# Block-sparse attention with a gated MoE on one core: weight pieces, key copies and x copies in other places of the order, and 64-column value products

## The chip, the core and the metric

The kernel runs on one core of a Trainium2 chip. The metric is device microseconds of one execution, the median of three runs. The engines are named as in the profile: PE (TensorE matmul), PEld (its weight load), DVE (VectorE), ACT (ScalarE), POOL (GpSimd) and SP (SyncE, which here only issues DMAs).

## What is computed

```python
# B, H, S, D = 4, 8, 768, 64; blocks of 32 rows, 24 of them; w_val, w_out 512x512, conv_w 5x512
scores = q @ k.T / 8                    # kept where the mask holds
mask = |blk_i - blk_j| <= 1, or i or j is the first or the last block, or blk_j is one of 3 sampled for blk_i
x = softmax(scores) @ v                 # all heads side by side: x is 4 x 768 x 512
gate = sigmoid(causal 5-tap convolution of x with conv_w, column by column)
out = (gate * (x @ w_val)) @ w_out
```

## The kernel before

**Units.** Batches 0 and 1 are the first group, 2 and 3 the second. A *place* is a pair of query blocks in both batches of a group; places -1 and -2 are the first and last block of one batch each, which see all keys (the global places). `ORDER` lists 13 places for each group, each place has two units, so there are 52 units; unit n of the text is step n of the main loop (line 887). Units 0 to 25 are the first group, with the global ones at 18 to 21 and places 9 and 10 at 22 to 25.

**A step of the loop.** In step n PE computes the scores of unit n (`scores`, tile `sc`), DVE their row maxima (`mx`), ACT the exponentials (`pe`, four instructions). For unit n-1 PE transposes the exponentials (`pt`, two tiles) and ACT copies each to SBUF (`ptr`); for unit n-2 PE multiplies by the values (`values`, tile `av`, from the own keys' values `va` and the gathered ones `vb`), DVE divides (`rs`, `x`), PE transposes x (`turn`, `xp`) and ACT copies it to `xT` (`finish`). One call of `values` for a place makes 32 matmuls of 32 columns. Every engine works strictly in the order in which the code is written (class `InOrder`), so an instruction that waits holds back all behind it on its engine.

**Queries.** `qc` tiles, 3 of them, come by DMA from SP; ACT scales each (group 0) `SCALE_AHEAD` = 2 units ahead of its first use.

**Weights.** w_val and w_out come as 8 pieces of 512 KB in 64-bit words, each issued by SP in a step set by `WEIGHTS_AT`, into four staging tiles (`wst`) that are later the buffers of xh, xl, yh and yl. `decode` turns one into a high part and a rest: four DVE instructions (`words<-wst`, two on `wst`, `words<-words,wst`), an ACT cast (`wv` or `wo`, high part) and a POOL subtraction (rest). `prepare` advances this in every step of the loop, once behind each of the two `pt` tiles: one DVE instruction in the first half, two in the second, so three a unit; so a piece's cast can come to stand between the two `ptr` copies. Only when all pieces are decoded do the gates of the MoE begin (`gates`, 16 instructions `th` on DVE for a tile of rows, ACT ahead of and behind them).

**The MoE.** When all x of a row tile are in `xT`, it is queued for gates, for its split into xh (ACT) and xl (POOL), and for `project`: products `vp` with w_val, gating on DVE, yh (ACT), yl (POOL), products `op` with w_out. `fill` puts these PE pieces between the attention's from unit 16 on, at the pace of `PACE`.

**Keys.** A place's 12 key blocks stand in `kg` (2 tiles). The group's keys are in SBUF (`keys`); POOL copies from there, except that for places 9 and 10 of the first group and for the first place of the second (`FROM_HBM`) SP fetches the sampled blocks (6 DMAs a place, and 2 more for the second group's first place) from memory. The keys of the second group are loaded in units 22 and 23 (`KEYS_AT`).

Of the kernel before, what the change touches and what calls it, by code (L numbers as in the profile page):

```python
# [22 lines left out]
DV = D + 1  # L23
# [12 lines left out]
ORDER = (1, 2, 0, 3, 4, 5, 6, 7, 8, -1, -2, 9, 10)  # L36
KEYS_AT = (22, 22, 23, 23, 23, 23)
QRING = 3
# [32 lines left out]
def steps(n, half):  # L71
    return 2 if half or n >= 14 else 1

# [5 lines left out]
def attention_moe(ctx, tc, qb, kb, v, vp, sampled, w_val, conv_w, w_out, ident_in, slot_in, out):  # L79
# [140 lines left out]
    decoded = set()  # L220

    def decode_weights():

        yield from decode(cwp[:, 0, :], cwp[:, 1, :], cst, CH * KW)
        dve.tensor_tensor(
            out=cw.rearrange("p c k -> p (c k)"), in0=cwp[:, 0, :].bitcast(F32), in1=cwp[:, 1, :].bitcast(F32),
            op=ALU.add,
        )
        for n in range(2 * CH):
            dst = wv if n < CH else wo  # L230
            while len(staged) <= n or step[0] < staged[n][0] + (DECODE_LAG if n else FIRST_LAG):
                yield False
            yield from decode(dst[0][:, n % CH, :], dst[1][:, n % CH, :], staged[n][1], DM)
            decoded.add(n)
        decoded.add("all")

# [263 lines left out]
    def values(un):  # L500
# [14 lines left out]
        else:  # L515
            slots = [(a, h, b, (4 * a + 2 * b + h) * DV) for a in range(2) for h in range(2) for b in range(2)]
            own = pr.pl.va[:, pr.i]
            rest = pr.pl.vb.rearrange("p j (e d) -> p j e d", e=EACH)[:, :, pr.i]
            for a, h, b, hd in slots:
                for c in range(2):  # L520
                    for j in range(2):
                        rows = slice(64 * b + BLK * j, 64 * b + BLK * j + BLK)
                        vt = rest[:, j, :] if c else own
                        matmul(
                            pr.av[rows, a, h, :], un.PT[4 * h + 2 * a + c][:, rows], vt[:, hd : hd + DV],
                            start=c == 0, stop=c == 1, tile_position=(0, rows.start),
                        )
# [204 lines left out]
    def queue_rows(bt, t):  # L732
        m = Rows()
        m.bt, m.tile, m.w, m.begun, m.pending, m.gated, m.need = bt, t, WIDTHS[t], False, False, 0, 0
        to_gate.append((m, gates(m)))
        to_split.append((m, split(m)))

    def prepared(m):
# [22 lines left out]
    def prepare(steps):  # L761
        for _ in range(steps):
            if next(decoding, None):
                continue

            if to_gate and (to_gate[0][0].begun or len(gating) < 2):
                m = to_gate[0][0]
                if not m.begun:
                    m.begun = True
                    gating.add(id(m))  # L770
                advance(to_gate)

# [114 lines left out]
    for n in range(N + LAG_V):  # L887
        step[0] = n
        if n == 0:
            begin()  # L890
        else:
            while more_queries(n):
                pass
            while more_own(n):
# [12 lines left out]
        if n:  # L907
            until("scaled", n + SCALE_AHEAD, scale, "queries")
        store()
# [5 lines left out]
        if n == 0:  # L915
# [5 lines left out]
            begin_second()  # L921
        until("early", n + COPY_AHEAD, copy_early, "keys")
        if n < AT_ONCE:
# [7 lines left out]
        mine = units[n - LAG_V].pr if 0 <= n - LAG_V < N and units[n - LAG_V].last else None  # L931
        if mine is not None and not any(k >= N or units[k].pl.glob for k in (n + 1, n + 2)) and not completes(mine):
# [18 lines left out]
        if 0 <= n - LAG_T < N:  # L951
            for half, _ in enumerate(transposes(units[n - LAG_T]) if n > LAG_T else range(2)):
                if half == 1:
                    ends_of_pairs()
                for _ in range(2):
# [3 lines left out]
                crowded = half and n > LAG_T and units[n - LAG_T].pl.glob and units[min(n + 1, N - 1)].pl.glob  # L959
                prepare(1 if crowded else steps(n, min(half, 1)))  # L960
                settle()
        else:
            fill()
            ends_of_pairs()
            prepare(steps(n, 0))
# [56 lines left out]
```

## Time and profile before

| | |
|---|---|
| median of 3 runs (369.94, 368.28, 369.55) | 369.55 us |
| the profiled execution | 366.96 us |
| its span | 365.2 us |
| PE busy | 343.1 us, 94% |
| DVE, ACT, POOL busy | 254.0, 241.9, 158.0 us |
| granted TensorE clock, mean | 0.998 |

All durations below are of the profiled execution, which was 2.6 us faster than the median of the runs. PE is the busiest engine by far. In the page's timeline of 40 slices PE's digits are 8 or below only in the first slices, up to about 90 us, and at the end.

### The profile page before, as it was taken

To read this page: it belongs to the slowest core of one execution; us is meant where nothing else is said; L and a number is where in the kernel's file an instruction comes from. 1 tells how busy PE (TensorE), PEld (TensorE's weight loads), DVE (VectorE), ACT (ScalarE), POOL (GpSimd) and SP (SyncE) were. 2 spreads that over 40 slices of the span, in tenths; PEclk is the share of its full clock that TensorE was granted. 3 is DMA by queue.
4 is the path that set the end of the run, shared out by engine and by line. 5 is a ranking of instruction groups with operands and counts; after the bars stand their busy time and mean duration, and the time that the engine had idled before them with its cause. 6 is when DMAs were issued, how large, how long until landed. Compare 5 with 4: busy or idle time off the path is not lost.

```text
span 365.2 us, 15814 instructions
## 1 busy us (share of the span) xinstructions
PE 343.1 (94%) x6628; PEld 270.7 (74%) x6628; DVE 254.0 (70%) x543; ACT 241.9 (66%) x564; POOL 158.0 (43%) x232
## 2 busy tenths in 40 slices
PE   8899888778999999999999999998999999998995
PEld 7576565457877888777787778876779778987883
DVE  4666797968976964399599845698569542989720
ACT  2769696697877875686868766686667855635321
POOL 0373494943235012677248831455004810645540
PEclk9999999999999999999999999999999999999999
DMA  7987888874981798776624666345515001020202
GB/s 271 370 265 270 277 272 274 292 220 113 334 305 44 243 384 242 256 211 196 202 79 145 180 206 208 87 154 203 175 65 177 4 31 61 0 83 4 88 0 87
DMA packets 32122, 64.60 MB, mean 177 GB/s; under 512 B 4659, under 2 KB 16052, under 8 KB 31924
## 3 DMA queue, kind: packets, MB, share of 16 engines
q1 hardware_dynamic: 31762, 63.51, 52.9%
q8 instruction: 52, 0.85, 0.9%
q14 instruction: 18, 0.15, 0.1%
q10 hardware_dynamic: 290, 0.09, 0.1%
HBM read 57.29 MB, written 6.29 MB: 174 GB/s over the span
## 4 chain that ended last, share of the span: by engine, by line
PE 62%; DVE 17%; DMA 7%; ACT 6%; SPq 3%; issue 3%; POOL 1%; ACTq 0%; DVEq 0%; POOLq 0%
PE op L97 15%; PE vp L97 12%; PE av L97 12%; PE pt L97 10%; DVE th L97 10%; PE sc L97 8%; DVE mx L97 4%; DMA qc<-in_q 4%; PE xp L97 3%; DMA wst<-in_w_out 3%; SPq L97 2%; PE s L97 2%; ACT pe L97 2%; ACT ptr L97 2%; DMA wst<-in_w_val 1%
## 5 line engine op out<-in xcount | busy, mean ns | idle before, releaser
L97 DVE SCALAR_TENSOR_TENSOR th<-xT,cw,th 128x388 f32<-128x388 f32 (+1 forms) x128 | 98.2, 782 | 20.6 <-ACT th L97 18.4
L97 POOL COPY kg<-keys 128x256 f32 (+2 forms) x155 | 77.1, 542 | 42.6 <-PE sc L97 15.8
L97 ACT ACTIVATE pe<-sc,mx 128x256 f32<-128x256 f32 x176 | 68.9, 475 | 39.2 <-DVE mx L97 39.0
L97 POOL TENSOR_TENSOR yl<-th,yh 128x384 fp32r<-128x384 f32 x32 | 36.2, 1132 | 116.1 <-ACT yh L97 92.7
L97 DVE TENSOR_REDUCE mx<-sc 128x2 f32<-128x512 f32 x88 | 56.4, 681 | 38.1 <-PE sc L97 36.0
L97 ACT COPY ptr<-pt 128x512 f32<-128x512 f32 x112 | 65.5, 602 | 16.1 <-PE pt L97 15.9
L97 PE MATMUL av<-va,ptr 128*32 128x65 f32 x1664 | 55.1, 224 | 4.9 <-ACT ptr L97 3.5
L97 PEld LDWEIGHTS av<-va,ptr 128*32 128x32 f32 x1664 | 41.0, 109 | 25.0 <-ACT ptr L97 13.1
L97 PE MATMUL sc<-kg,qc 64*32 64x256 f32 x1408 | 54.7, 382 | 4.8 <-ACT pe L97 2.2
L97 PE MATMUL av<-vb,ptr 128*32 128x65 f32 x1920 | 57.0, 220 | 0.6 <-issue 0.3
L97 PE MATMUL op<-wo,yh 128*128 128x512 f32 x192 | 53.8, 402 | 0.0
L97 PE MATMUL vp<-xh,wv 128*128 128x384 f32 (+1 forms) x256 | 52.3, 346 | 1.1 <-DVE th L97 0.7
L97 PE MATMUL pt<-ident,pe 128*128 128x128 f32 x352 | 49.6, 275 | 1.2 <-ACT rest L97 1.2
L97 PEld LDWEIGHTS av<-vb,ptr 128*32 128x32 f32 x1920 | 46.2, 109 | 5.0 <-issue 4.5
L97 PEld LDWEIGHTS vp<-xh,wv 128*128 128x128 f32 x256 | 43.9, 189 | 2.0 <-PE vp L97 1.0
L97 PEld LDWEIGHTS pt<-ident,pe 128*128 128x128 f32 x352 | 40.2, 140 | 4.7 <-ACT rest L97 1.5
L97 POOL TENSOR_TENSOR xl<-xT,xh 128x384 fp32r<-128x384 f32 (+1 forms) x32 | 35.8, 1133 | 16.3 <-ACT xh L97 16.3
L97 PEld LDWEIGHTS sc<-kg,qc 64*32 64x32 f32 x1408 | 23.8, 106 | 24.7 <-issue 7.4
L97 PEld LDWEIGHTS op<-wo,yh 128*128 128x128 f32 x192 | 34.8, 188 | 6.9
L97 PE MATMUL op<-wo,yl 128*128 128x512 f32 x96 | 31.5, 409 | 0.4 <-POOL yl L97 0.4
L97 DVE SCALAR_TENSOR_TENSOR th<-th,vp 128x384 f32<-128x384 f32 (+2 forms) x48 | 18.5, 413 | 17.0 <-PE vp L97 14.8
L97 ACT CAST yh<-th 128x384 fp32r<-128x384 f32 x32 | 16.8, 524 | 18.9 <-DVE th L97 18.7
(60 smaller groups left out, 391.4 us busy)
## 6 DMA issues: line engine op xcount, KB each, us to landing
vb<-in_v SPq DMA_DIRECT2D x140, 130.0 KB, 3.8
qc<-in_q SPq DMA_DIRECT2D x21, 256.0 KB, 3.4
out<-ot SPq DMA_DIRECT2D x20, 256.0 KB, 2.1
vb<-in_v SPq DMA_DIRECT2D x18, 260.0 KB, 5.4
keys<-in_k SPq DMA_DIRECT2D x9, 512.0 KB, 4.0
va<-in_vp SPq DMA_DIRECT2D x8, 520.0 KB, 5.3
vb<-in_v SPq DMA_DIRECT2D x8, 520.0 KB, 5.9
va<-in_vp SPq DMA_DIRECT2D x14, 260.0 KB, 4.0
```

The lines of the kernel that those rows point to most:

```text
L97: made = getattr(self.eng, name)(*args, **kwargs)
```

## The change

- The first two weight pieces are issued in step 2 by POOL, between two of its key copies, and no longer by SP in steps 2 and 4; the others are issued by SP in steps 4, 5, 7, 8, 9 and 10.
- In steps 0 to 15 `prepare` runs only behind both `ptr` copies; in steps 5, 6 and 7 (`EAGER`) it runs four instructions, a whole piece, in others three.
- In steps up to 6 the queries are scaled one unit ahead, and not two.
- `FROM_HBM` is empty: POOL copies all sampled keys on chip, for which copies of units 16 to 25 are queued up to 6 units ahead. The keys of the second group are issued two a step in units 22 and 23, four in 22.
- From step 16 on an x that is already transposed is copied to `xT` behind the first `ptr` copy and no longer behind the second, and fewer transposes of x are put off to the next step. Gates start when a row tile is queued.
- In batches 0 and 1 the products with the own keys' values take 64 columns at once: 8 matmuls of 64 columns, then 16 of 32 columns, instead of 32 of 32 columns that alternate between the two sources.

```diff
-KEYS_AT = (22, 22, 23, 23, 23, 23)
+WIDE = 2
+KEYS_AT = (22, 22, 22, 22, 23, 23)
...
-WEIGHTS_AT = (2, 4, 5, 6, 8, 9, 10, 11)
+WEIGHTS_AT = (2, 2, 4, 5, 7, 8, 9, 10)
+MIDWAY = 2
+EAGER = (5, 6, 7)
 DECODE_LAG = 2
-FIRST_LAG = 3
 SCALE_AHEAD = 2
+EARLY = 6
...
+def copy_ahead(n):
+    return 6 if 16 <= n < 20 else COPY_AHEAD
...
-FROM_HBM = ((9, 10), ORDER[:1])
+FROM_HBM = ((), ())
...
-    return 2 if half or n >= 14 else 1
+    return 2 if half or n >= 14 or n in EAGER else 1
...
-            sp.dma_start(flat, (w_val if n < CH else w_out).bitcast(I32)[c * 128 : (c + 1) * 128, :])
+            (pool if n < MIDWAY else sp).dma_start(flat, (w_val if n < CH else w_out).bitcast(I32)[c * 128 : (c + 1) * 128, :])
...
-            while len(staged) <= n or step[0] < staged[n][0] + (DECODE_LAG if n else FIRST_LAG):
+            while len(staged) <= n or step[0] < staged[n][0] + (DECODE_LAG if n >= MIDWAY else 3):
...
+            wide = pr.bt.b < WIDE
+            if wide:
+                for a, h, b, hd in slots:
+                    matmul(
+                        pr.av[64 * b : 64 * b + 64, a, h, :], un.PT[4 * h + 2 * a][:, 64 * b : 64 * b + 64],
+                        own[:, hd : hd + DV], start=a + h == 0, stop=False, tile_position=(0, 64 * b),
+                    )
             for a, h, b, hd in slots:
-                for c in range(2):
+                for c in range(1 if wide else 0, 2):
...
+        if len(to_gate) == 1:
+            begin_gates()
...
-        if k < 2 * CH and n >= WEIGHTS_AT[k] and (k < 4 or k - 4 in decoded):
+        if MIDWAY <= k < 2 * CH and n >= WEIGHTS_AT[k] and (k < 4 or decoded_at.get(k - 4, n) < n):
...
-            until("scaled", n + SCALE_AHEAD, scale, "queries")
+            until("scaled", n + (SCALE_AHEAD if n > EARLY else 1), scale, "queries")
...
-        until("early", n + COPY_AHEAD, copy_early, "keys")
+        until("early", n + copy_ahead(n), copy_early, "keys")
+        if n == MIDWAY:
+            copy_some(4)
+            for _ in range(MIDWAY):
+                next(weights)
...
-        def ends_of_pairs():
+        def ends_of_pairs(half):
             nonlocal mine
-            if mine is not None:
+            if half == 0 and n < SPARE:
+                return
+            if half and mine is not None:
...
-                if half == 1:
-                    ends_of_pairs()
+                ends_of_pairs(half)
...
-                prepare(1 if crowded else steps(n, min(half, 1)))
+                if n < SPARE:
+                    prepare(steps(n, 0) + steps(n, 1) if half else 0)
+                else:
+                    prepare(1 if crowded or ahead and half else steps(n, min(half, 1)))
```

The order of ACT's instructions around unit 6, before, from the scaling of `qc` (`wv` is a piece's high part, `xT` the transposed x):

```order
L97 ACTIVATE qc<-qc 128x512
L97 ACTIVATE pe<-sc,mx 128x256 x4
L97 COPY ptr<-pt 128x512
L97 CAST wv_127<-words 128x512
L97 COPY ptr<-pt 128x512
L97 COPY xT_691<-xp 128x4x64
```

And after, at the same unit:

```order
L106 COPY xT_545<-xp 128x4x64
L106 CAST wv_127<-words 128x512
L106 ACTIVATE pe<-sc,mx 128x256 x4
L106 COPY ptr<-pt 128x512 x2
L106 COPY xT_668<-xp 128x4x64
L106 CAST wv_127<-words 128x512
L106 ACTIVATE qc<-qc 128x512
L106 ACTIVATE pe<-sc,mx 128x256 x4
```

The cast has moved behind both `ptr` copies and the copy of x; the scaling of the queries stands one unit later, and there is a piece in each of two units in a row.

ACT again, at units 24 and 25, behind the global places, before:

```order
L97 ACTIVATE pe<-sc,mx 128x256 x4
L97 COPY ptr<-pt 128x512
L97 CAST yh<-th 128x384
L97 COPY ptr<-pt 128x512
L97 COPY xT_1922<-xp 128x4x32 x2
L97 COPY xT_1922<-xT_691 128x4x4
L97 ACTIVATE pe<-sc,mx 128x256 x4
L97 COPY ptr<-pt 128x512
L97 CAST yh<-th 128x384
L97 COPY ptr<-pt 128x512
L97 COPY xT_1819<-xp 128x4x64
```

And after:

```order
L106 ACTIVATE pe<-sc,mx 128x256 x4
L106 COPY ptr<-pt 128x512
L106 COPY xT_1823<-xp 128x4x32 x2
L106 COPY xT_1823<-xT_668 128x4x4
L106 CAST yh<-th 128x384
L106 COPY ptr<-pt 128x512
L106 ACTIVATE pe<-sc,mx 128x256 x4
L106 COPY ptr<-pt 128x512
L106 COPY xT_1729<-xp 128x4x64
L106 CAST yh<-th 128x384
```

The copies of x stand ahead of the cast and of the second `ptr` copy.

SP's issues from the piece ahead of unit 8's queries, before:

```order
L97 DMA wst<-in_w_val 128x1024
L97 DMA qc<-in_q 128x2x256
L97 DMA va_125<-in_vp 64x1040
L97 DMA wst<-in_w_val 128x1024
L97 DMA vb<-in_v 32x2x1040
L97 DMA vb<-in_v 32x4160 x6
L110 TENSOR_LOAD sv
L97 DMA qc<-in_q 128x2x256
L97 DMA va_126<-in_vp 64x1040
L97 DMA wst<-in_w_out 128x1024
```

And after:

```order
L106 DMA wst<-in_w_val 128x1024
L106 DMA qc<-in_q 128x2x256
L106 DMA va_125<-in_vp 64x1040
L106 DMA vb<-in_v 32x2x1040
L106 DMA vb<-in_v 32x4160 x6
L119 TENSOR_LOAD sv
L106 DMA wst<-in_w_out 128x1024
L106 DMA qc<-in_q 128x2x256
L106 DMA va_126<-in_vp 64x1040
L106 DMA wst<-in_w_out 128x1024
```

A place's stretch of SP has one piece or two as before, but w_val is through one piece earlier. POOL issues the two pieces in step 2 behind its first static key copies. In units 15 to 19 POOL now has, between yl, xl and static copies, 16 single key copies of places 9 and 10; the 9 of the second group's first place come in units 24 and 25, with yl between them.

## Rows read from the trace of the kernel before

**Rows 1.** The page: busy time, share of the span and instructions of each engine.

```profile
PE 343.1 (94%) x6628; PEld 270.7 (74%) x6628; DVE 254.0 (70%) x543; ACT 241.9 (66%) x564; POOL 158.0 (43%) x232
```

**Rows 2.** Stretches: length; busy of PE, PEld, DVE, ACT, POOL; clock, DMA share, GB/s.

```profile
19.74:74.22 54.48, 47.34 (x1276) 33.23 (x1275) 42.80 (x93) 40.38 (x97) 35.68 (x62) 1.00 0.82 272
74.22:88.04 13.82, 10.31 (x226) 7.52 (x225) 10.20 (x20) 13.03 (x34) 7.05 (x6) 1.00 0.58 174
...
88.04:152.91 64.87, 64.16 (x1392) 51.67 (x1391) 45.12 (x96) 45.15 (x104) 18.77 (x24) 1.00 0.76 251
```

**Rows 3.** PE's timeline, scores of units 4 and 5: start, us, instruction, count.

```profile
24.06 1.09 PE L97 MATMUL sc<-kg,qc 64*32 64x256 f32 x32
...
27.39 0.62 PE L97 MATMUL sc<-kg,qc 64*32 64x256 f32 x2
```

**Rows 4.** ACT's timeline, unit 4; in brackets the idle time before and its releaser.

```profile
27.33 0.63 ACT L97 ACTIVATE qc<-qc 128x512 f32<-128x512 f32 x1 [2.25 <-DMA qc<-in_q]
27.86 1.55 ACT L97 ACTIVATE pe<-sc,mx 128x256 f32<-128x256 f32 x4
```

**Rows 5.** DVE's timeline, maxima of unit 4, and the units around 45 us.

```profile
25.24 1.29 DVE L97 TENSOR_REDUCE mx<-sc 128x2 f32<-128x512 f32 x2 [1.43 <-PE sc L97]
...
44.65 1.27 DVE L97 TENSOR_REDUCE mx<-sc 128x2 f32<-128x512 f32 x2
...
46.58 0.49 DVE L97 TENSOR_SCALAR wst<-wst 128x512 uint32<-128x512 uint32 x1
...
48.60 1.28 DVE L97 TENSOR_REDUCE mx<-sc 128x2 f32<-128x512 f32 x2
```

**Rows 6.** Waits: who waits, for what: total us, count, longest.

```profile
ACT qc L97 <- DMA qc<-in_q: 9.5, 7, 2.5
DVE words L97 <- DMA wst<-in_w_val: 2.5, 2, 1.9
DVE words L97 <- DMA wst<-in_w_out: 2.1, 2, 1.1
```

**Rows 7.** SP's timeline: DMA issues of places' queries, a weight piece and gathered values.

```profile
23.23 0.38 SPq L97 DMA_DIRECT2D qc<-in_q  x1
...
33.17 0.58 SPq L97 DMA_DIRECT2D wst<-in_w_val  x1
33.84 4.88 SPq L97 DMA_DIRECT2D vb<-in_v  x7
...
75.23 0.33 SPq L97 DMA_DIRECT2D qc<-in_q  x1
```

**Rows 8.** PE's timeline, unit 16: two waits.

```profile
82.40 0.34 PE L97 MATMUL av<-va,ptr 128*32 128x65 f32 x8 [1.57 <-ACT ptr L97]
...
85.56 0.44 PE L97 MATMUL xp<-ident,x 128*128 128x128 f32 x2 [1.23 <-DVE x L97]
```

**Rows 9.** PE's scores of units 24, 25 and 27, and ACT's copy at unit 25.

```profile
133.75 1.46 PE L97 MATMUL sc<-kg,qc 64*32 64x256 f32 x32
...
140.48 1.06 PE L97 MATMUL sc<-kg,qc 64*32 64x256 f32 x22 [0.30 <-issue]
...
153.76 1.09 PE L97 MATMUL sc<-kg,qc 64*32 64x256 f32 x30 [0.24 <-ACT xT L97]
...
140.18 0.44 ACT L97 COPY xT<-xp 128x128 f32<-128x128 f32 x2
```

**Rows 10.** Chain of waits: pieces of `av` on PE, a global unit's and a usual unit's.

```profile
129.19 1.50 PE av L97 x96
...
149.05 1.07 PE av L97 x64
```

**Rows 11.** Groups on POOL: busy us, mean ns | idle before, releasers.

```profile
L97 POOL COPY kg<-keys 128x256 f32 x105 | 49.9, 510 | 17.2 <-PE sc L97 15.8 <-PE pt L97 1.4
...
L97 POOL TENSOR_TENSOR yl<-th,yh 128x384 fp32r<-128x384 f32 x32 | 36.2, 1132 | 116.1 <-ACT yh L97 92.7 <-PE vp L97 23.4
```

**Rows 12.** The page's DMA issues: count, KB each, us from issue to landing.

```profile
vb<-in_v SPq DMA_DIRECT2D x18, 260.0 KB, 5.4
```

More of the change, by code (lines that the diff above doesn't have):

```diff
@@ L215, in load_weights @@
             c = n % CH
[L216 removed]
+            (pool if n < MIDWAY else sp).dma_start(flat, (w_val if n < CH else w_out).bitcast(I32)[c * 128 : (c + 1) * 128, :])
             staged.append((step[0], flat.rearrange("p (n w) -> p n w", w=2)))
             yield
[L220 removed]
+    decoded, decoded_at = set(), {}
     def decode_weights():
@@ L234, in decode_weights @@
             decoded.add(n)
+            decoded_at[n] = step[0]
         decoded.add("all")
@@ L525, in values @@
                             pr.av[rows, a, h, :], un.PT[4 * h + 2 * a + c][:, rows], vt[:, hd : hd + DV],
-                            start=c == 0, stop=c == 1, tile_position=(0, rows.start),
+                            start=c == 0, stop=a + h == 2 if wide else c == 1, tile_position=(0, rows.start),
                         )
@@ L736, in queue_rows, with begin_gates @@
         to_split.append((m, split(m)))
+        if len(to_gate) == 1:
+            begin_gates()
+    def begin_gates():
+        m = to_gate[0][0]
+        m.begun = step[0]
+        gating.add(id(m))
+        advance(to_gate)
     def prepared(m):
@@ L767, in prepare @@
                 m = to_gate[0][0]
[L768 to L771, printed above, removed]
+                if m.begun:
+                    if step[0] > m.begun or step[0] > 2 * SPARE:
+                        advance(to_gate)
+                else:
+                    begin_gates()
         if {CH, CH + 1} <= decoded and len(staged) == 2 * CH and to_split and unread <= {id(to_split[0][0])}:
@@ L893, in attention_moe @@
                 pass
-            while more_own(n):
+            while n > 1 and more_own(n):
                 pass
         k = len(staged)
-        if k < 2 * CH and n >= WEIGHTS_AT[k] and (k < 4 or k - 4 in decoded):
+        if MIDWAY <= k < 2 * CH and n >= WEIGHTS_AT[k] and (k < 4 or decoded_at.get(k - 4, n) < n):
             next(weights)
@@ L931, in attention_moe @@
         mine = units[n - LAG_V].pr if 0 <= n - LAG_V < N and units[n - LAG_V].last else None
-        if mine is not None and not any(k >= N or units[k].pl.glob for k in (n + 1, n + 2)) and not completes(mine):
+        if mine is not None and not any(k >= N or units[k].pl.glob for k in (n + 1, n + 2)) and not (n < SPARE and completes(mine)):
             waiting.append(mine)
             mine = None
-        def ends_of_pairs():
+        def ends_of_pairs(half):
             nonlocal mine
-            if mine is not None:
+            if half == 0 and n < SPARE:
+                return
+            if half and mine is not None:
                 turn(mine)
@@ L959, in attention_moe @@
                 crowded = half and n > LAG_T and units[n - LAG_T].pl.glob and units[min(n + 1, N - 1)].pl.glob
-                prepare(1 if crowded else steps(n, min(half, 1)))
+                crowded = crowded and to_gate and to_project and to_project[0][0] is not to_gate[0][0]
+                ahead = 2 * SPARE - 2 < n < 40 and to_gate and to_project and to_project[0][0] is not to_gate[0][0]
+                if n < SPARE:
+                    prepare(steps(n, 0) + steps(n, 1) if half else 0)
+                else:
+                    prepare(1 if crowded or ahead and half else steps(n, min(half, 1)))
                 settle()
```

2 lines of the change are left out of this document (1 added, 1 removed).

## The prediction

> **What bounds the kernel now.** I read the page's busy times first: PE has 94% of the span [rows 1], so nearly everything is PE work, and a change that leaves PE's work as it is can win only where PE stands still. The table of stretches says where that is [rows 2]. From 19.74 to 88.04 us (scores of unit 3 to scores of unit 17) PE is busy for 47.34 + 10.31 = 57.65 of 54.48 + 13.82 = 68.30 us. From 88.04 to 152.91 us it is busy for 64.16 of 64.87. So the change can win in the first stretch by less waiting, and behind it only in small stalls, some of which busy time hides, since a stretched record counts in full.
>
> How fast could a unit of the first stretch be? Units 4 and 5 show one that PE alone paces: scores to scores 27.39 - 24.06 = 3.33 us [rows 3]. The twelve units from 19.74 to 74.22 take 54.48 us [rows 2], 4.54 each. So something else sets the pace, and three things compete:
>
> - DVE. From the start of the row maxima to the first of three decode instructions is 46.58 - 44.65 = 1.93 us, the three take 48.60 - 46.58 = 2.02 us, and there the next maxima start without a break [rows 5]. A unit with three decode instructions costs DVE 3.95 us.
> - SP. Between 31 and 50 us it issues DMAs with hardly a gap: the piece at 33.17 (0.58 us), then seven issues of gathered values in 4.88 us [rows 7]. The queries of one place are issued at 23.23 us and those of the sixth place behind it at 75.23 us [rows 7]: 52.00 us for 6 places, 12 units, so 4.33 us a unit. The gathered values, not the queries, fill that time.
> - ACT, which waits for these queries: 9.5 us in 7 waits, the longest 2.5 us [rows 6]. At 27.33 us it has waited for 2.25 us, and the exponentials of unit 4, whose maxima began at 25.24, start only at 27.86 [rows 4, 5].
>
> DVE's waits for weight pieces are 2.5 and 2.1 us [rows 6]. All these lie beside each other on different engines, so they can't be added up; the slowest queue is the floor that is left when they go.
>
> **The change part by part.** The sum is made against the profiled execution, 366.96 us (span 365.2 and 1.8 around it), which lies 2.59 us under the median of 369.55; the saving found is then taken from the median.
>
> Units 3 to 14. The queries for unit 6 are scaled in step 5 and no longer in step 4, where they had come 2.25 us late. Without that, the exponentials of unit 4 could start when the first of two maxima is there, about 25.24 + 1.29/2 = 25.9, not at 27.86: 1.9 us. What is late next is SP's own pace. The two pieces that leave SP are two issues of about 0.55 us, 1.1 us in all. The new floor for the twelve units is SP's 52.00 - 1.1 = 50.9 us, against 54.48: **-3.6 us**. DVE allows it: a unit with a whole piece decoded costs about 1.93 + 2.02 + 0.49 (a fourth instruction, taken as the shortest shown) = 4.4 us, close to SP's pace, and only units 5, 6 and 7 have one. The least is what the first wait gives back if all later ones remain, cut by half for what units 5 to 7 lose by decoding more each, 1.0 us; the most is with SP no bound and DVE the floor, 12 x 3.95 + 3 x 0.49 = 48.9, so 5.6 us.
>
> Units 15 and 16. They take 13.82 us [rows 2], of which 2 x 3.33 would be bare units and one product with w_val lies in them besides. There PE waits 1.57 us for a `ptr` copy behind a cast of wo, a gate and two xh casts, and 1.23 us for x, behind gates on DVE [rows 8]. Decoding ends a unit sooner, so the cast of wo is gone from there, but four gate instructions stand in unit 15 where two stood. I take back a third of the 2.8 us: **-0.9 us**, between +0.7 (the two gate instructions more, taken like a decode instruction at 2.02/3 = 0.67 each [rows 5], show up by half) and -2.8.
>
> Copies of x from unit 18 on. Scores of unit 25 start at 139.53, and 22 of 32 records come only from 140.48 on, when ACT, at 140.18, has made the copy of x that frees their buffer [rows 9]. A set of scores takes 1.09 [rows 3]; this one ends at 141.5, 0.9 us late. The same shows at unit 24 (1.46 instead of 1.09 [rows 9]) and at unit 27, where 30 of 32 records wait until 153.76 although the first two started at 152.91: 0.85 us. Together 2.1 us, on PE's path, since PE is full there. With the copy behind the first `ptr` copy, a transpose and a copy sooner, all three go: **-2.1 us**, at the least 0 (the transpose of that x itself may be late), at the most 2.8, with smaller ones of the kind. What is late next is the second `ptr` copy, pushed back by 0.44 us [rows 9] or a little more; the products that read it stand behind the next scores, 1.09 us, which hides it.
>
> Wide products. No row shows a 64-column product of this kind. A usual unit's `av` piece is 1.07 us with 64 records, a global one's 1.50 with 96 [rows 10]: (1.50 - 1.07)/32 = 13.4 ns a record and 0.21 us that doesn't depend on the number. If four of the narrow tiles stream beside each other, two of the double width do, and 8 wide matmuls take as long as the 16 they replace. So streaming saves nothing, and a change of shape in the middle may cost another 0.2 us. In units 3 to 14 SP's pace covers it. In the seven such units of the stretch where PE is full it doesn't: 7 x 0.2 = **+1.4 us**. The ends: +4.6 with all 22 units (22 x 0.21), and -4.6, if the 0.21 us were the price of alternating between two sources rather than of starting. I take the one nearest to the rows, a start for each shape.
>
> The Trainium skill, page "TensorEngine Tiling (Array Packing)", section "Key Properties", says that changing the tiling mode, not just the tile, drains TensorE. The rows agree as far as they go, with 0.21 us for each `av` piece behind scores of another shape, but no run here shows a switch inside `av`. By that rule alone the sum would gain the whole +4.6 us wherever PE sets the pace, and this is the first rival below.
>
> Key copies. POOL gets 16 + 9 copies of 0.51 us and a few static ones, about 14 us, in a stretch in which it is busy for 18.77 of 64.87 us [rows 2, 11]. SP loses as many DMAs. They cost nothing by themselves. But `op` pieces start a unit sooner and need yl, which now stands behind copies: 0 to 1.7 us (three copies and a TENSOR_LOAD), I take **+0.9**. The nine copies for the second group, 9 x 0.51 = 4.6 us, need its keys, which now come two steps' issues sooner at best; POOL's 64.87 - 18.77 = 46 idle us leave them room.
>
> Behind 152.91 us, and in the tail from 310 us on, the order of PE, DVE and ACT is the same but for the copies of x. 0.
>
> Sum: -3.6 - 0.9 - 2.1 + 1.4 + 0.9 = -4.3 us. 366.96 - 4.3 = 362.7 for a profiled execution of that kind, and for the median 369.55 - 4.3 = **365.2 us**.
>
> **The rivals.** Measurement can tell about 0.5% here, 1.8 us.
>
> *No change (367.7 to 371.4), about 369.* Either the extra change of shape costs 0.21 us in each of the 22 units, because PE and not SP is what ends last there: -4.3 - 1.4 + 4.6 = -1.1, so 368.5. Or the pieces don't do what the edit says: issued by POOL behind four key copies they are no sooner in SBUF than by SP, and DVE still waits 4.6 us for pieces, SP's pace is unbroken and only the copies of x pay: -2.1 + 2.3 = +0.2, so 369.8. For it: no DMA of this kind of POOL is in the trace. Against: the first piece is decoded three units after its issue, some 13 us, while 260 KB of gathered values land 5.4 us after their issue [rows 12].
>
> The Trainium skill, page "SBUF — State Buffer", section "SBUF: two separate sides", has a rule for that second case: descriptors of a DMA issued by GpSimd are written by GpSimd, and while VectorE holds the shared port they can't be. It gives some 3.1 us instead of 0.62 us for one transfer. No run here shows it yet; at that size it would be hidden under the 13 us.
>
> *More (359 to 363), about 360.* SP's pace isn't a floor, because its issues themselves wait for buffers that units free. Then DVE is the floor, -5.6 for the twelve units, -2.8 for units 15 and 16, and the change of shape is free: -5.6 - 2.8 - 2.1 + 0.9 = -9.6, so 360.0. For it: SP's seven issues take 0.70 us each [rows 7], longer than the queries' 0.38, which can be back-pressure. Against: the DMA share is already 0.82 there [rows 2].
>
> *Slower (over 371.4), about 374.* yl on POOL. A key copy waits for PE to be through with the buffer: 15.8 us of POOL's idle time before these copies is `PE sc` [rows 11]. POOL is in order, so a yl behind such a copy waits too, and `op` and all of PE behind it. If the 16 copies of places 9 and 10 are in front of yl whenever it is due, that is 16 x 0.51 = 8.2 us in the place of the 0.9: -4.3 - 0.9 + 8.2 = +3.0, so 372.6, and 374 with a third of the other nine copies (4.6/3 = 1.5). It decides when a copy's buffer is freed later than yh is cast. Against: the copies are queued up to six units ahead, and yl had 92.7 us of slack waiting for ACT's yh [rows 11].
>
> **How the numbers follow.** Forecast (363 to 367.7): 0.54. More: 0.16. No change: 0.18. Slower: 0.12. The likeliest gives 365.2. The range leaves out the slower case, and of "no change" its upper part: 359.0 to 369.6. Faster by over 0.5%, that is under 367.7, is the forecast and "more": 0.70; within 0.5%: 0.18; slower: 0.12.
>
> **What would show it.** Right: the scores of unit 17 start at about 83.5 us instead of 88.04; the idle time of ACT before `qc` falls from 9.5 to about 6 us, with none in step 4; no cast of wv or wo between two `ptr` copies of a unit; SP still busy without gaps between 23 and 70 us; the scores of units 24, 25 and 27 without a break; `av` pieces of the chain at about 1.3 us, and the stretch that was 64.87 us long about as long. Wrong: DVE waits for `wst` of the POOL pieces; `av` at 1.1 or under (wide is free, more is won) or over 1.5; PE waiting for yl for more than 2 us in all; pieces from SP still late, with units 8 to 14 at 4.5 us each.

## The result: the kernel after is slower by 0.9%

| | before | after |
|---|---|---|
| median (9 runs of each, in turn) | 368.76 us | 371.10 us |
| ratio of the two | | 1.0087, 95% interval 1.0059 to 1.0115 |
| the profiled execution | 366.96 us | 372.53 us |
| its span | 365.2 us | 370.8 us |
| mean granted clock of the profiled execution | 0.998 | 0.994 |

The forecast was 365.2 us, 359.0 to 369.6, and faster at 0.70. It was wrong in its sign. Both profiled executions lie at an end of their runs, before 1.8 us under the median and after 1.4 us over it, so 3.2 of the 5.6 us between the spans belong to those two executions and not to the change.

The busy times of after answer to [rows 1]:

```profile
PE 346.0 (93%) x6276; PEld 272.0 (73%) x6276; DVE 250.1 (67%) x543; ACT 241.5 (65%) x564; POOL 165.6 (45%) x253
```

PE has 352 matmul records fewer and is busy 2.9 us longer. Where the time lies is told by the stretches from the scores of unit 3 to those of unit 17, of unit 17 to 21, and of unit 21 to 51; first after, then before (length; busy PE, PEld, DVE, ACT, POOL; clock, DMA share, GB/s):

```profile
19.29:87.74 68.45, 59.46 (x1275) 41.87 (x1274) 54.41 (x115) 53.80 (x130) 47.37 (x77) 0.98 0.77 251
87.74:117.91 30.17, 27.58 (x518) 21.74 (x517) 20.07 (x46) 20.67 (x45) 12.89 (x18) 1.00 0.46 156
117.91:302.55 184.64, 179.55 (x3782) 143.10 (x3781) 126.17 (x276) 129.22 (x308) 76.94 (x122) 1.00 0.51 167
```

```profile
19.74:88.04 68.30, 57.65 (x1500) 40.75 (x1499) 53.00 (x112) 53.40 (x130) 42.73 (x68) 1.00 0.78 252
88.04:115.29 27.25, 26.84 (x566) 21.38 (x565) 21.10 (x45) 20.04 (x44) 9.22 (x10) 1.00 0.70 228
115.29:297.76 182.47, 179.34 (x3845) 142.89 (x3844) 130.42 (x279) 130.36 (x309) 77.73 (x118) 1.00 0.55 174
```

The first stretch is as long as before in these two executions. The second is 2.92 us longer, the third 2.17, and the tail from unit 51 to the end 0.81 (370.8 - 302.55 against 365.2 - 297.76). The later stretches hardly differ between executions of one kernel, or of kernels with the same order there; the first one differs by some us (64.3 to 68.5 in the variants below that have the order of after up to step 15). So I compare behind unit 17 from the traces, and the first stretch by medians. Behind unit 17 after loses 5.90 us, or 4.6 if a second profile of the kernel before is taken for the first (experiment 12). The medians differ by 2.34. If that loss is in each run, a median run of after comes to unit 17 some 2.3 to 3.6 us sooner than one of before. That is an estimate. The profiles fit it: before has unit 17 at 88.04 and 88.00 us, and of the eight kernels below with wide products and the new order of the first steps (after, and experiments 1, 3, 4, 5, 9, 10 and 11) five have it at 84.4 to 84.8, the others at 87.1 to 89.1.

**What the first stretch shows.** Unit 9 is the worst of it: queries that come late hold ACT, ACT's exponentials hold the buffers of the scores, and the clock that is granted falls. ACT and PE at unit 9 (timeline), and the stretch of that unit:

```profile
45.79 0.63 ACT L106 ACTIVATE qc<-qc 128x512 f32<-128x512 f32 x1 [1.80 <-DMA qc<-in_q]
...
47.20 1.09 PE L106 MATMUL sc<-kg,qc 64*32 64x256 f32 x30 [2.08 <-ACT pe L106]
```

```profile
44.49:52.72 8.23, 5.88 (x92) 4.20 (x91) 5.00 (x13) 5.21 (x13) 4.85 (x9) 0.79 0.79 261
```

PE waited 2.08 us, and then worked for part of the unit at 1.2 GHz instead of 2.4 (mean 0.79). The wait at step 4 [rows 4] is gone, and ACT's waits for queries fell from 9.5 to 4.1 us, but this one stayed (1.78 us in unit 9 before).

**What the second stretch shows.** In unit 18 PE did this before (timeline):

```profile
96.00 0.66 PE L97 MATMUL pt<-ident,pe 128*128 128x128 f32 x4
96.42 1.63 PE L97 MATMUL vp<-xh,wv 128*128 128x384 f32 x8
97.88 0.86 PE L97 MATMUL vp<-xl,wv 128*128 128x384 f32 x4
98.58 0.60 PE L97 MATMUL pt<-ident,pe 128*128 128x128 f32 x4
```

And after, in units 18, 19 and 20:

```profile
98.08 0.66 PE L106 MATMUL pt<-ident,pe 128*128 128x128 f32 x4
99.71 0.66 PE L106 MATMUL pt<-ident,pe 128*128 128x128 f32 x4 [0.97 <-ACT rest L106]
...
106.77 0.66 PE L106 MATMUL pt<-ident,first 128*128 128x128 f32 x4 [0.82 <-ACT rest L106]
...
115.49 0.66 PE L106 MATMUL pt<-ident,first 128*128 128x128 f32 x4 [0.54 <-ACT rest L106]
```

Gates start earlier, so a product with w_val is ready half a step sooner. PE takes one of them already at the end of unit 17, and from then on each stands behind the second transposes of its unit and no longer between the first and the second. There it had covered the time in which DVE and ACT make the exponentials of a global unit's second half. Nothing covers it now.

**What the third stretch shows.** Unit 31 is 1.1 us longer, units 42 and 43 1.2 us each; units 26 to 28 are 0.6 us shorter. Unit 24 is 1.0 us longer and unit 25 0.8 shorter, which comes with the wide products (experiment 6). Three rows (ACT at unit 31, PE at unit 31 and at the end of unit 42):

```profile
177.28 0.41 ACT L106 COPY xT<-xp 128x256 f32<-128x256 f32 x1
...
179.64 0.34 PE L106 MATMUL av<-va,ptr 128*32 128x65 f32 x8 [1.17 <-ACT ptr L106]
...
246.48 0.41 PE L106 MATMUL xp<-ident,x 128*128 128x128 f32 x2 [0.82 <-DVE xT L106]
```

At unit 31 the copy of x and a gate that starts with it stand ahead of ACT's second `ptr` copy, for which PE's value products wait (0.39 us before). In step 42 PE transposes an x that the kernel before had transposed in step 41; the next transpose, at 246.48, then waits until DVE has set a buffer to zero behind a gate instruction. In unit 43 the scores behind it take 1.74 us for 1.09, and the value products wait 0.34 us for `ptr`.

### The profile page after: what moved, and what is told of

Its sections match the earlier page's. It is cut to its first block, busy times and chain, and to the rows that moved or that the text cites. A ratio compares the mean times of both kernels' runs of the same rounds, so it can differ in the third digit from the quotient of the medians.

```text
span 370.8 us, 15072 instructions
## 1 busy us (share of the span) xinstructions
PE 346.0 (93%) x6276; PEld 272.0 (73%) x6276; DVE 250.1 (67%) x543; ACT 241.5 (65%) x564; POOL 165.6 (45%) x253
## 4 chain that ended last, share of the span: by engine, by line
PE 59%; DVE 19%; ACT 8%; DMA 7%; issue 4%; POOL 1%; SPq 0%; POOLq 0%; ACTq 0%; DVEq 0%
PE vp L106 13%; DVE th L106 12%; PE av L106 12%; PE op L106 12%; PE pt L106 10%; PE sc L106 7%; DVE mx L106 4%; ACT pe L106 3%; PE xp L106 3%; PE s L106 3%; ACT ptr L106 2%; DMA wst<-in_w_out 2%; DMA va<-in_vp 2%; DMA keys<-in_k 2%; DMA qc<-in_q 1%
## 5 line engine op out<-in xcount | busy, mean ns | idle before, releaser
L106 POOL COPY kg<-keys 128x256 f32 (+2 forms) x174 | 84.4, 530 | 52.3 <-DMA va<-in_vp 27.7
L106 DVE SCALAR_TENSOR_TENSOR th<-xT,cw,th 128x388 f32<-128x388 f32 (+1 forms) x128 | 95.9, 754 | 8.0 <-ACT th L106 5.2
L106 POOL TENSOR_TENSOR yl<-th,yh 128x384 fp32r<-128x384 f32 x32 | 35.3, 1103 | 104.6 <-ACT yh L106 104.6
L106 PEld LDWEIGHTS av<-va,ptr 128*32 128x32 f32 (+1 forms) x1312 | 35.4, 117 | 24.8 <-ACT ptr L106 12.1
L106 PE MATMUL av<-va,ptr 128*32 128x65 f32 (+1 forms) x1312 | 46.9, 226 | 4.9 <-ACT ptr L106 2.8
L106 PE MATMUL av<-vb,ptr 128*32 128x65 f32 x1920 | 47.8, 223 | 0.3 <-DMA vb<-in_v 0.3
L106 PEld LDWEIGHTS av<-vb,ptr 128*32 128x32 f32 x1920 | 37.8, 110 | 5.2 <-issue 3.3
```

Source lines behind the costliest of these rows:

```text
L106: made = getattr(self.eng, name)(*args, **kwargs)
```

## The experiments

Each was timed in turn with the kernel before; ratios are to that one. "Behind 17" is the time from the scores of unit 17 to those of unit 51, 209.72 us before and 214.81 after. PE's *breaks* are idle times of over 0.2 us before which the profile finds nothing that PE waited for ("issue").

**1. The products back between the transposes.**

```diff
-                    if filled[0] + 1 <= due(n, min(half, 1) + 1):
+                    if not (half and 17 <= n <= 19) and filled[0] + 1 <= due(n, min(half, 1) + 1):
```

> The kernel after, but in steps 17, 18 and 19 no PE product of the MoE is put behind the second transposes, so that in steps 18 to 20 each stands between the first and the second transposes again, as in the kernel before. Theory A (the products that moved a unit forward left the transposes of the global units uncovered): the three new waits of PE for ACT's exponentials (0.97, 0.83 and 0.54 us at 99.71, 106.77 and 115.49) and the wait of 0.26 us for yl go, so about 2.3 to 2.6 us less than the kernel after, and the time comes to about that of the kernel before. Theory B (the time goes in the wide products and in the first 17 units, and the waits of the global units are only passed on): less than 1 us is won, and units 18 to 22 together stay 2.5 us longer than before.

1.0017 (0.9986 to 1.0048), and behind 17 213.05 us: 1.8 us of the 2.3 to 2.6 expected. The three waits for exponentials are gone. A new one took part of it: in unit 20 the last scores wait for a copy of x that stands behind the second `ptr` copy.

```profile
104.81 0.67 PE L106 MATMUL s<-keys,qc 64*32 64x256 f32 x16 [1.05 <-ACT xT L106]
```

So the uncovered transposes are 1.8 us of the loss, net.

**2. All value products narrow.**

```diff
-WIDE = 2
+WIDE = 0
```

> The kernel after with all value products 32 columns wide, in the order of the kernel before. Theory A (a change of shape inside the products costs a fixed 0.14 us: the pieces are 1.21 us long after and 1.07 before): in the seven units of batches 0 and 1 from unit 17 on where PE is full 1.0 us is won, in units 3 to 16 between nothing and 2.0 us, so 1 to 3 us less than after. Theory B (the first units are paced by queries, decoding and values, and the 0.14 us stand beside other waits): 1 us and no more. Theory C (fewer instructions also spare PE's instruction fetch): the kernel gets slower than after.

1.0122 (1.0066 to 1.0177): slower than after, if anything, the one thing that only theory C expected. The pieces did get shorter, 1.07 us for 1.21. The waits of PE from 19 to 87 us, largest first, show what came instead:

```profile
PE av L106 <- issue: 5.4, 5, 1.8
PE xp L106 <- DVE x L106: 1.5, 1, 1.5
PE xp L106 <- issue: 1.4, 1, 1.4
PE sc L106 <- POOL kg L106: 1.1, 2, 0.9
PE pt L106 <- issue: 0.7, 1, 0.7
```

7.5 us of breaks in 7 places; after has none there. They fall into the middle of runs of small matmuls:

```profile
31.28 0.24 PE L106 MATMUL av<-vb,ptr 128*32 128x65 f32 x1 [1.78 <-issue]
...
57.55 0.24 PE L106 MATMUL av<-vb,ptr 128*32 128x65 f32 x1 [1.26 <-issue]
...
72.90 0.33 PE L106 MATMUL xp<-ident,x 128*128 128x128 f32 x1 [1.43 <-issue]
```

The trace has a DMA queue of its own for instructions (before, whose products are narrow too, then after; section 3 of the page):

```profile
q8 instruction: 52, 0.85, 0.9%
...
q8 instruction: 50, 0.82, 0.9%
```

All 9 breaks of this kernel, those around 140 us too, end 1.2 to 1.6 us after the end of one of its transfers of 16 KB, and so do 42 of the 43 breaks in all fourteen profiles. The places of the breaks tell more. Number the records of PE's own stream in order: matmuls, weight loads and its sequencer's instructions. In the same 42 cases 193 or 194 records stand between the last multiple of 256 and the matmul at which the break ends, and there is one transfer to some 256 records. None of these 42 matmuls waits for a semaphore. The 43rd, at 44.49 us in experiment 7 (0.24 us), stands elsewhere and waits for one. So in 42 breaks PE had run out of instructions: the profile has no other cause that would come every 256 records.

What the breaks cost is another question. Up to unit 17 this profile takes 66.96 us, and that of after, with no break there but with the wait at unit 9, 68.45. The breaks stand beside other waits, and the 7.5 us are not their price.

**3. The copies of x as before.**

```diff
-            if half == 0 and n < SPARE:
+            if half == 0:
                 return
...
-        if mine is not None and not any(k >= N or units[k].pl.glob for k in (n + 1, n + 2)) and not (n < SPARE and completes(mine)):
+        if mine is not None and not any(k >= N or units[k].pl.glob for k in (n + 1, n + 2)) and not completes(mine):
```

> The kernel after with the copies of x and their transposes where the kernel before has them: behind the second copy of the transposed exponentials, and never put off where a row tile is completed. Theory A (the copies gain where they freed a buffer for the scores, and lose where they push back the second copy of the exponentials or set a buffer to zero behind a gate): units 26 to 28 get 1.5 us longer, units 31, 43 and 44 get 3.5 us shorter, so 2 us less than after, most of it behind 170 us. Theory B (the copies are worth the 2.1 us of the forecast): 1.5 to 2.1 us more than after.

1.0016 (0.9974 to 1.0058), about 2 us under after, as theory A had it. Behind 17 213.36 us. Units 26 to 28 get 0.8 us longer (5.10, 7.13 and 5.91 for 4.88, 6.28 and 6.14), unit 31 8.63 for 9.73, units 42 and 43 4.73 and 6.15 for 5.95 and 7.36. The copies as the change has them cost 1.45 us behind unit 17, where the forecast had them win 2.1.

**4. Sampled keys from memory again.**

```diff
-FROM_HBM = ((), ())
+FROM_HBM = ((9, 10), ORDER[:1])
...
-KEYS_AT = (22, 22, 22, 22, 23, 23)
+KEYS_AT = (22, 22, 23, 23, 23, 23)
```

(and `copy_ahead` always 2.)

> The kernel after with the sampled keys of places 9 and 10 of the first group and of the first place of the second group fetched from memory by SP again, and the second group's keys issued and the copies queued as before. Theory A (the copies on POOL are hidden, and fewer DMAs help little): within 0.7 us of after. Theory B (key copies ahead of yl and the keys that now come in a row ahead of the values hold PE up around 110 and 138 us): 1.2 us less, the 0.26 us wait for yl at 110 and the 1.0 us break in the products of unit 22 at 138 gone.

1.0031 (0.9997 to 1.0065): 1.3 us under after, but not by theory B's way: behind 17 it has 215.68 us, 0.9 more than after, the wait for yl is still there (0.27 us), and the break at unit 24 is longer. What is less lies in the first stretch, 64.30 us, whose order this edit doesn't touch. In kernels with the order of after in the first steps that stretch is 64.3 to 68.5 us long, so one profile of each can't tell whether the edit has a part in it. It stays open.

**5. Three repairs at once**: two gate instructions in step 15, no product behind the second transposes in step 19, early copies of x in steps 16 to 29 alone.

```diff
+                    if not (half and n == 19) and filled[0] + 1 <= due(n, min(half, 1) + 1):
...
-                    prepare(steps(n, 0) + steps(n, 1) if half else 0)
+                    prepare((2 if n == 15 else steps(n, 0) + steps(n, 1)) if half else 0)
...
-            if half == 0 and n < SPARE:
+            if half == 0 and not SPARE <= n < 30:
...
-        if mine is not None and not any(k >= N or units[k].pl.glob for k in (n + 1, n + 2)) and not (n < SPARE and completes(mine)):
+        if mine is not None and not any(k >= N or units[k].pl.glob for k in (n + 1, n + 2)) and not (not SPARE <= n < 30 and completes(mine)):
```

> The kernel after with three repairs: only two decode or gate instructions in step 15 and no product behind the second transposes in step 19, so that the MoE's products stand where the kernel before has them in units 17 to 21; and the early copies of x only from step 16 to 29, behind that as before. From the scores of unit 17 to those of unit 51 the kernel before takes 209.72 us and the kernel after 214.81. Theory A (the loss behind unit 17 is the uncovered transposes of the global units, 2.9 us, and the copies of x at units 31, 43 and 44, 3.5 us): both go but for some 0.5 us, so about 209 to 210 us there; with the first 17 units 2 to 4 us sooner than before, the time is 1.5 to 3.5 us under that of the kernel before. Theory B (the loss is work that comes back elsewhere): more than 212 us there, and no better than before.

0.9912 (0.9878 to 0.9945), 365.09 us, and behind 17 210.41. Theory A holds: 4.4 of the 5.1 us that after loses there are those two causes.

**6. The kernel before with wide products alone** (the lines of `values` in the diff).

> The kernel before with only the value products of batches 0 and 1 made wide. Theory A (a wide unit costs PE 0.14 us, and nothing else depends on it): the units 17 to 19 and 24 to 27 get 0.14 us longer each, 1.0 us in all, and the time 0 to 1 us more than before. Theory B (PE waits for its own instructions where DMA is busy, and 8 matmuls fewer a unit spare it such breaks): the breaks of PE without a releaser, 1.34 us at 72.87, 0.34 at 67.39 and 0.30 at 140.48 before, get fewer, and the time is the same or up to 2 us less, although each piece is longer.

0.9939 (0.9906 to 0.9973), 365.79 us: what cost time by the forecast is the best part of the change. The pieces are longer, as A says (unit 17 takes 5.57 us for 5.44); but PE has no break at all up to unit 17. Its waits from 19 to 87 us:

```profile
PE av L98 <- ACT ptr L98: 4.1, 9, 1.8
PE xp L98 <- DVE x L98: 1.0, 1, 1.0
PE sc L98 <- ACT pe L98: 0.4, 1, 0.4
PE xp L98 <- ACT pe L98: 0.3, 1, 0.3
```

Unit 25 takes 7.65 us, as in after, where the kernel before took 8.42 and 8.67 in its two profiles. The copies of x stand here as they do before, so it is not they that made it shorter. Unit 24 has a break of 1.26 us in exchange.

That fewer instructions are the whole reason is not shown. The stretch up to unit 17 has some ten transfers of instructions with wide products and twelve with narrow ones, and they also fall on other places of the order; no run separates the two.

**7. The kernel before with the part for the first 16 units alone**: pieces by POOL, decoding behind both copies, `EAGER`, `EARLY`; with two gate instructions in step 15 and no product behind the second transposes in step 19, so that PE's order is that of before.

> The kernel before with only the part for the first 16 units: two weight pieces by POOL, decoding behind both copies and a piece at once in steps 5 to 7, queries scaled one unit ahead up to step 6; PE's order is that of the kernel before. Theory A (this part pays, and the kernel after loses it behind unit 17): the scores of unit 17 come 1.5 to 4 us sooner than in runs of before, the rest takes 209.7 us to unit 51 as before, and the time is 1.5 to 4 us less. Theory B (SP's issues and DMA set the pace of these units whatever the decoding does): within 1 us of before.

1.0003 (0.9977 to 1.0029). Theory B's number, but not its reason: PE breaks for 4.0 us up to unit 17, and 1 us behind the first break the clock falls to 1.2 GHz (PE at unit 5, then that unit's stretch):

```profile
32.88 0.24 PE L99 MATMUL av<-vb,ptr 128*32 128x65 f32 x1 [2.33 <-issue]
```

```profile
29.08:36.08 7.00, 4.67 (x107) 3.54 (x107) 3.37 (x8) 4.04 (x10) 0.00 (x0) 0.84 0.93 314
```

Unit 5 takes 7.00 us (3.48 with the same part and wide products, in after and in experiment 9). All ten timed runs of this kernel have a mean clock of 0.984 to 0.995.

**8. Narrow products, and the gathered values of places 3 to 8 left out.**

```diff
+        if 3 <= pl.vseq < 9:
+            pl.vb = places[2].vb
+            return
         pl.vb = three.tile([128, 2, EACH * H * DV], F32, tag="vb", name="vb")
```

> The kernel after with narrow value products, and with the gathered values of places 3 to 8 left out (units 6 to 17 use those of the third place, so SP issues eight DMAs fewer for each of six places). Only the times of units 6 to 17 count. Theory A (SP's issues are the floor of these units): without them the unit's time falls from 4.5 to DVE's 4.0 us or less. Theory B (PE's breaks without a releaser, 7.5 us in all in the narrow kernel up to unit 17, are instruction fetches that come late because the DMA engines are busy): the breaks between 35 and 75 us go or shrink to less than 0.3 us each. If the breaks stay as they are with the DMA share far lower, theory B falls.

Stretches from 42 to 80 us, first here, then in experiment 2:

```profile
42.00:80.00 38.00, 35.77 (x966) 24.92 (x965) 35.39 (x73) 32.93 (x82) 29.39 (x42) 0.96 0.44 133
```

```profile
42.00:80.00 38.00, 31.94 (x897) 22.56 (x884) 33.03 (x69) 31.40 (x77) 27.94 (x41) 1.00 0.81 264
```

With DMA at 0.44 instead of 0.81 the breaks end: the last is at 41.89 us, while experiment 2 has five more, 5.3 us in all, from 46 to 73. Units 9 to 15 take 28.11 us for 31.58, 4.0 each, which is DVE's cost. Theory B holds, as far as one execution tells, and A can't be told from it here: the breaks alone are more than the 3.5 us won.

**9, 10 and 11. What is left if only the good parts stay.** 9 is before with the edits of 6 and 7. 10 spreads the second group's keys over four steps. 11 adds the early copies of x for steps 23 to 28.

```diff
-KEYS_AT = (22, 22, 23, 23, 23, 23)
+KEYS_AT = (22, 23, 23, 24, 24, 25)
...
+            if half == 0 and not 23 <= n < 29:
+                return
...
+        if mine is not None and not any(k >= N or units[k].pl.glob for k in (n + 1, n + 2)) and not (not 23 <= n < 29 and completes(mine)):
```

> The kernel before with the wide value products and the part for the first 16 units, and nothing of the key copies and the copies of x. Theory A (the part for the first units pays once PE has fewer instructions to fetch: alone it gave nothing, with breaks of PE of 2.33, 0.51 and 0.97 us without a releaser): the scores of unit 17 come at 84 to 85 us, 1.5 us or so sooner than with wide products alone (86.42), the rest to unit 51 takes 210.0 us as there, and the time is 1 to 2 us less than with wide products alone, about 1% less than before. Theory B (the first units are paced by SP's issues and DMA, wide products have already taken what there was): within 0.7 us of wide products alone.

0.9885 (0.9841 to 0.9928), 364.64 us, some 1.1 us under wide products alone by the medians; the intervals of the two overlap. Theory A is likelier by that, not shown. Its profiled execution (368.2 us) is the slowest of its six and came to unit 17 only at 89.11, so that the 84 to 85 us expected stand unconfirmed there; those of 10 and 11, with the same order up to that point, have 84.82 and 84.42.

> The same, with the keys of the second group issued over steps 22 to 25 (one, two, two, one) and no longer in 22 and 23. Theory A (PE's break in the value products of unit 22, 1.0 us in the kernel after and 0.7 to 1.4 us in every variant with wide products, is an instruction fetch held up by the 3 MB of keys): the break goes or falls under 0.4 us, units 24 and 25 together take 0.7 to 1.0 us less, with no wait for keys after it. Theory B (the break belongs to the place in the program): it stays at 0.7 to 1.4 us.

0.9872 (0.9828 to 0.9916), 363.53 us. PE at unit 24 in 9, then in 10:

```profile
137.17 0.63 PE L100 MATMUL av<-va,ptr 128*64 128x65 f32 x14 [0.70 <-issue]
```

```profile
132.59 0.62 PE L100 MATMUL av<-va,ptr 128*64 128x65 f32 x14 [0.41 <-issue]
```

The break shrinks but stays; units 24 and 25 take 13.90 for 14.18 us. That is less than theory A wanted: the eight DMAs of sampled keys for the second group's first place are issued there, and DMA is busy all the same.

> The same again, with the copies of x behind the first copy of the transposed exponentials in steps 23 to 28 alone. Theory A (there they free a buffer for the scores and push nothing back): units 26 to 28 take 0.8 us less (the kernel after has 17.30 us for the three, before 17.85), units 31, 43 and 44 as before. Theory B (what is won at units 26 to 28 comes back at 29 to 31): nothing.

0.9870 (0.9837 to 0.9903), 363.45 us. Units 26 to 28 take 17.29 us for 18.15 in 10, as A says, and the break at unit 24 is gone, but unit 37 takes 6.76 for 6.12 and unit 30 3.66 for 3.34: behind 17 209.30 for 209.62, and the median is the same. So theory B came true in part: some of what is won comes back, at unit 30 and at unit 37, which it didn't name. Why the break is gone here and not in 10 was not tried. 10 and 11, not told apart by their times, are the fastest versions, 1.3% under before.

**12. The kernel before once more.**

> The kernel before, unchanged, profiled once more: its profile was taken of an execution of 366.96 us, 1.7 us under the median. Theory A (narrow products make PE wait for instruction fetches in the first 17 units, by an amount that differs from run to run): behind unit 17 all is as in the first profile (209.7 us to unit 51), and up to unit 17 breaks of PE without a releaser of 1 to 6 us in all, where the first profile has 1.7 us; a slower execution has more of them or a lower granted clock. Theory B (wide products save elsewhere): breaks as in the first profile, under 2 us, whatever the time.

1.0006 (0.9965 to 1.0046) against itself. Its profiled execution (368.14 us, near the median) waits for instructions much longer than the first one (PE's waits from 19 to 88 us, here, then in the first profile):

```profile
PE av L97 <- issue: 2.2, 3, 1.1
...
PE xp L97 <- issue: 1.7, 1, 1.7
...
PE pt L97 <- issue: 0.9, 1, 0.9
```

```profile
PE xp L97 <- issue: 1.3, 1, 1.3
...
PE av L97 <- issue: 0.3, 1, 0.3
```

4.9 us in 5 breaks against 1.7 in 2. Over all profiles, the four with narrow products and the gathered values have 1.7, 4.9, 4.0 and 7.5 us of breaks up to unit 17, the nine with wide ones 0 six times, and 0.8, 1.4 and 1.5. Behind 17 it has 210.97 us, 1.25 more than the first profile. Of that 0.85 us is one break, at the same matmul, that grew from 0.31 us (109.28) to 1.16 (110.13). So the loss of after behind unit 17 depends on the execution of before that it is held against: 5.1 us against the first, 3.8 against this one.

## Why the prediction was wrong

**The first 16 units: the direction right, the cause half right.** The step "-3.6 - 0.9" is not far from the 2.3 to 3.6 us of the estimate above. The profile of after missed its mark, "about 83.5 us" for unit 17: it has 87.74, with the wait at unit 9. But alone the part is worth nothing (experiment 7), on top of wide products about 1 us (9 against 6), and wide products alone about 3 us: experiment 6 is 2.8 us faster in the medians (2.3 by its ratio), though it takes 0.3 us more behind unit 17 than the first profile of before. The sum had SP's 4.33 us a unit as the floor that was left, and 50.9 us for units 3 to 14. No run shows that floor by itself; those units take 55.1 us in after, 51.4 to 52.0 in experiments 1, 4, 10 and 11, and 52.6 with wide products alone. What the sum lacked is in its own row [rows 2]: a DMA share of 0.82 with PE's breaks beside it. Two breaks stood in the trace of before, 1.34 and 0.34 us with the releaser "issue", and I listed them under nothing.

**Wide products: the price right, the sign wrong.** I took 0.2 us a unit for the change of shape and found 0.14 us more for a unit's piece, in the chain of waits of unit 17, which answers to [rows 10]:

```profile
88.84 1.21 PE av L106 x48
```

The Trainium skill, page "TensorEngine Tiling (Array Packing)", section "Key Properties", has the drain for a change of mode; a fixed price of a switch agrees with it, but no run separates the switch from the wide matmuls themselves. The failure is that the sum, and the rival, counted what the matmuls cost and not what their number costs. With 176 matmuls fewer (352 records) PE stands still for its instructions less often: up to unit 17 for 0 to 1.5 us, with narrow products for 1.7 to 7.5. The kernel before is 2.3 us faster with that alone (experiment 6, 1.0 to 3.5 us by its interval).

**Copies of x: the rows misread.** I took the pause of the scores of unit 25, to 140.48, for a wait for ACT's copy at 140.18 [rows 9]. The row says "issue", the matmul there waits for no semaphore, and it stands at one of the places every 256 records, as the breaks of the second profile of before (0.55 us) and of experiments 2 and 7 (1.13 and 0.55 us) at the same place do. One of the two copies in ACT's row did end at 140.45, but the matmul has no wait for it. The same goes for the slow scores of unit 24: with narrow products such a place lies in the middle of them, and in experiments 6 and 9, whose copies are those of before, they take 1.09 us. So the 0.9 us at unit 25 and the 0.4 at unit 24 were instructions; only the wait at unit 27 was the copy's. Without the early copies (experiment 3) units 23, 26 and 27 get longer, by 0.2, 0.2 and 0.85 us, and unit 28 shorter by 0.2: that much of the 2.1 us was there, 1.1 us net. And "what is late next is the second `ptr` copy ... which hides it" fails at unit 31, where the copy of x brings a gate with it (1.1 us), and at 42 and 43 (2.4 us), where that transpose comes a step later. So the step "-2.1" measured +1.45 us (experiment 3).

**The step that decides the sign was not in the sum.** "The order of PE ... is the same" was meant for the time behind 152.91 us, but for units 17 to 21 I saw that products come a unit sooner and asked only what they wait for (yl: 0.9 us, measured 0.26). I didn't ask what they had covered. 2.92 us were lost there, of which experiment 1 brings back 1.8 and experiment 5, where the products stand as before in these units, 2.3. The slower rival's mechanism, yl behind key copies, didn't happen; its time of 374 us is nearer than the forecast by chance. The measured 371.1 us even lies in the range of "no change", and that is chance too: the change of shape doesn't cost 0.21 us in each of 22 units, and DVE doesn't wait for the pieces that POOL issues.

**Smaller ones.** The POOL pieces: they land 4.8 us after their issue (median of the two), and DVE doesn't wait for them. The Trainium skill, page "SBUF — State Buffer", section "SBUF: two separate sides", has a lock of GpSimd's descriptors by VectorE. No run here tests it: POOL issues the two pieces from 22.23 to 23.46 us, and DVE works for 0.8 us of that and then stands idle until 25.74. The profile's DMA issues of after from 22 to 24 us:

```profile
wst<-in_w_val POOLq DMA_DIRECT2D x2, 512.0 KB, 4.8
```

The tail got 0.8 us longer, for which the sum had 0. It is as before in 9 to 11, which lack the early start of the gates and the new counts of their steps, and longer in 5, which has them; which of the two it is was not tried.

## What to carry to other kernels

When work becomes ready sooner, ask what stands in its old place: a product that fills PE while another engine prepares its next input is worth that wait, and moving it a half step ahead can cost more than all that made it ready. An idle time that has no releaser is a finding, not a remainder: count which instruction it stands at. Here it came every 256 records of PE, so it was PE's instructions, and fewer of them were worth a higher price each. And check of each wait you mean to remove that its releaser ends where the wait ends.

## What the runs showed of the hardware

- PE can run out of instructions. In these traces it breaks for 0.2 to 2.3 us in the middle of runs of small matmuls. 42 of 43 breaks end 1.2 to 1.6 us behind a transfer of 16 KB of the instruction queue, and 193 or 194 records behind a multiple of 256 in PE's own stream. The trace names no releaser.
- The breaks come where the DMA engines are busy: at 0.67 or more of their time in the 5 us before 42 of them (0.51 before the other, of 0.22 us). At a share of 0.44 (experiment 8, 42 to 80 us) there was none. Most transfers end without a break, at high shares too.
- Up to unit 17 the granted clock fell to 1.2 GHz for part of a unit behind idle times of PE of 1.8 to 2.8 us, and in experiment 12 behind 0.94 and 0.69 us; behind the 1.78 us break of experiment 2 it stayed at 2.4. Unit 5 of experiment 7, with a break of 2.33 us and such a fall, took 7.00 us, and 3.48 in experiment 9, the same kernel with wide products, which had neither there.
- A value piece of 64 narrow records takes 1.07 us, one of 16 records of 64 columns and 32 of 32 takes 1.21. Whether the 0.14 us are the change of shape is not shown.
